# Weight chunks decoded one by one, and x's smaller part by VectorE in every unit: a windowed attention with a gated block behind it

## The chip, the cores and the metric

The kernel runs on one NeuronCore of a Trainium2 chip. The time is device microseconds of one execution, as the median of several. TensorE (PE in the profile) multiplies matrices, VectorE (DVE), ScalarE (ACT) and GpSimd (POOL) work on elements, SyncE (SP) issues the DMAs. Each engine runs its own instructions in program order, and waits on semaphores for the others.

## The reference

For 8 batches and 8 heads of 576 positions with 64 dimensions each position attends to itself and the 63 before it; the result, with the heads side by side, is x (8 x 576 x 512). Then `h = relu(x @ w_in)` (512 to 1024), a convolution of three taps along the sequence for each of the 1024 columns, `gate = 1 / (1 + exp(-conv))`, and `(h * gate) @ w_out` (1024 to 512).

```python
scores = scale * np.matmul(q, k.transpose(0, 1, 3, 2))
mask = (rel >= 0) & (rel < window)
attn = softmax(np.where(mask, scores, -1e9))
x = np.matmul(attn, v)                      # heads side by side
h = np.maximum(x @ w_in, 0.0)
conv_out[s] = sum(conv_w[k] * h[s + k - 1] for k in range(3))
out = (h * sigmoid(conv_out)) @ w_out
```

## The kernel before

The 4608 rows of x are done in 12 units of 384 rows (`NX`), and every unit goes through attention, the product with w_in, the convolution with its gate, and the product with w_out. Units 0 and 1 are taken in halves of the 1024 columns: unit 0's first four chunks of 128 columns, unit 1's first four, unit 0's last four, unit 1's last four (`TASKS`, L44), so that the weights of the second half may come later; from unit 2 on a unit takes its eight chunks in a row.

**Split operands.** The products with w_in and w_out run on a reduced 32-bit type (fp32r). Each operand is held as a larger part, which that type holds exactly, and a smaller part, the rest; a product is three matrix products (larger by larger, larger by smaller, smaller by larger). For x a quarter of a unit (128 of the 512 columns) lies in a PSUM bank when `values` (L643) has multiplied the attention weights with v. `split_hi` (L648) copies the bank to `xh`, rounded. The smaller part `xl` comes about in two ways. For most units VectorE subtracts: `split_lo` (L653) reads the bank and `xh`. For the units in `BY_DIFFERENCE`, 1 and 2, TensorE subtracts in the bank itself, by a product of `xh` with the negated identity matrix (`less`, L657), and ScalarE or VectorE then copies the rest out (`split_rest`, L662). Either way the bank is free for other work only after the smaller part has been read.

**Weights.** w_in and w_out come as 64-bit numbers, as pairs of 32-bit words, in 16 chunks of 128 x 512. Decoding a chunk takes `magnitude` (L445 on ScalarE or L447), `shift` (L451, VectorE), `sign` (L455, VectorE), `low` (L458, ScalarE), `add_low` (L462, VectorE), then `larger` (L480) and `lo` (L485) for the two parts. w_in's chunks 0 and 1 are decoded alone, the other fourteen in pairs, each step once for 1024 columns (`DECODE`, L46). Two buffers `wx` take turns. The three taps (`cbits`, `cw`) are decoded by the same functions.

**Order of the work.** A planning function lists all pieces of work, and a table of numbers (`ORDER`) says in which order they are issued; a letter behind a number names the engine where there is a choice (A, D or P for ScalarE, VectorE, GpSimd), a figure after a slash the PSUM bank, and F*n* stands for *n* products on spare data that fill a gap. Every engine's instructions stand in the order of this table. There are eight banks.

**Other lines that matter.** `scores` (L554) multiplies q and k; `row_max` (L575) and `exps` (L585), `reciprocal` (L597) and `normalise` (L604) make the attention weights of a burst; `turn` (L611) and `unturn` (L616) transpose them for units 0 and 1. `mm1` (L669) is the product with w_in, `relu` L695/697, `conv_mid` L711/713 and `conv_side` L718 the taps, `sigmoid` L722, `gate` L729, `gate_hi` L734 and `gate_lo` L739 the split of h times gate, `mm2` L748 (L753 in the last unit) the product with w_out, `result` L758/761 the copy out of the bank.

Of the kernel before, what the change touches and what calls it, by code (L numbers as in the profile page):

```python
# [8 lines left out]
F32 = mybir.dt.float32  # L9
# [29 lines left out]

BY_DIFFERENCE = (1, 2)  # L40
# [84 lines left out]
def plan():  # L125
# [64 lines left out]
    at("minus")  # L190
# [64 lines left out]
    80A 77D 125 207P 222 215 82/6 239 223A 216P 86A 224 78 208/4 83A 142A 87 225P 217/5 84 198/0 81 232 438 143
    102/7 9 92 145 189 144 10 240 4 93 146 7 113/1 209A 231 147D 104A 148D 127A 226/6 439 443/2 190 115D 241 309
    128 149/7 130 129 242A 199A 116 218A 243 131 233A 114A 251/0 118A 152/1 151A 244P 445 440 2 310 154A 234 444
    164 235P 449 334 252D 165 446 119 245/4 153A 155 236/5 448 253 156 247/7 157D 237A 158 246A 132D 227A 254A
    120 F2/2 255/1 447 159 454/2 450A 133D 256A 248A 259/0 311A 607 117 441 257 455 121 260D 456 F2/5 261 249
# [103 lines left out]
def attention_moe(ctx: ExitStack, tc: tile.TileContext, q, k, v, first, w_in, conv_w, w_out, out):  # L363
# [100 lines left out]
    def part(buf, fs):  # L464
        return wx[buf][:, :len(fs) * DM]
# [409 lines left out]
```

## Time and profile before

| what | us |
|---|---|
| median of 3 runs | 509.57 (509.39 to 510.43) |
| profiled execution, its own time | 509.53 |
| span of the profiled execution | 507.8 |
| TensorE busy | 499.1 (98%), 5377 instructions |
| VectorE busy | 401.3 (79%), 1186 instructions |
| ScalarE busy | 315.5 (62%), 897 instructions |
| GpSimd busy | 149.1 (29%), 223 instructions |

The span runs from the first to the last recorded instruction; 1.7 us of the execution lie around it. A busy engine has an instruction in flight; consecutive instructions of one engine overlap a little in the record, so the length of one is somewhat more than what it adds. The chain of waits begins at the last instruction and goes back to what released each step, so that it shows which engine held up the end at each moment. A group names line, engine and operation, `out<-in`, shape, count, busy us, mean ns of one, and the idle time of the engine just before. The granted TensorE clock is 1.00 of full speed in every stretch shown.

### The profile page before, as it was taken

The numbers are of one execution on the slowest core, as the hardware profiler recorded it, in microseconds if no ns is written. First come the engines' busy times: TensorE is split into PE (matmuls) and PEld (weight loads), VectorE is DVE, ScalarE is ACT, GpSimd is POOL, SyncE is SP. The second block draws the span as 40 slices with busy tenths as digits, with TensorE's granted clock in tenths as the row PEclk, the third lists the DMA queues.
The fourth block names the chain that finished last, engine by engine and source line by source line (L and its number), as shares of the span: only waits on it lengthen the run. The fifth ranks groups of instructions, "written<-read, shape, count | busy, mean of one in ns | idle before, by whom it ended". The sixth has DMA issues, their size and how long they took to land.

```text
span 507.8 us, 13893 instructions
## 1 busy us (share of the span) xinstructions
PE 499.1 (98%) x5377; PEld 440.1 (87%) x5377; DVE 401.3 (79%) x1186; ACT 315.5 (62%) x897; POOL 149.1 (29%) x223
## 2 busy tenths in 40 slices
PE   8898999999999999999999999999999999999997
PEld 5687989888898898888898988989889889888996
DVE  6999999988877896787668887887887688683781
ACT  5999999979736752754767745924663763331150
POOL 4832440323240431331441230335125332203011
PEclk9999999999999999999999999999999999999999
DMA  8999438334364744416243737324444301600031
GB/s 309 346 345 346 151 110 267 112 93 130 110 186 128 203 133 126 131 62 203 78 154 82 243 95 227 97 70 117 144 159 142 102 1 55 207 21 2 0 125 62
DMA packets 27953, 72.04 MB, mean 142 GB/s; under 512 B 6128, under 2 KB 14448, under 8 KB 27888
## 3 DMA queue, kind: packets, MB, share of 16 engines
q1 hardware_dynamic: 27600, 69.59, 42.5%
q0 software_dynamic: 288, 1.57, 1.8%
q8 instruction: 42, 0.69, 0.6%
q14 instruction: 23, 0.19, 0.1%
HBM read 48.26 MB, written 11.01 MB: 117 GB/s over the span
## 4 chain that ended last, share of the span: by engine, by line
PE 92%; DVE 2%; ACT 2%; DMA 1%; POOL 1%; issue 0%; SPq 0%
PE bank L669 39%; PE bank L748 37%; PE bank L643 6%; PE bank L554 5%; PE bank L753 3%; ACT s L585 2%; DMA raw_in<-in_w_in_dram 1%; DVE c L718 1%; DVE s L575 1%; POOL s L604 0%; PE bank L657 0%; PE bank L611 0%; SPq L413 0%; POOL w_in L485 0%; DVE wx L462 0%
## 5 line engine op out<-in xcount | busy, mean ns | idle before, releaser
L669 PE MATMUL bank<-xh,w_in 128*128 128x384 f32 x768 | 196.6, 336 | 0.0
L748 PE MATMUL bank<-w_out,gh 128*128 128x512 f32 x528 | 168.8, 401 | 0.0
L669 PEld LDWEIGHTS bank<-xh,w_in 128*128 128x128 f32 x768 | 139.4, 188 | 6.4 <-ACT hbuf L695 0.6
L669 PE MATMUL bank<-xl,w_in 128*128 128x384 f32 x384 | 128.9, 336 | 0.0
L718 DVE SCALAR_TENSOR_TENSOR c<-hbuf,cw,c 128x386 f32<-128x386 f32 (+1 forms) x192 | 120.1, 651 | 4.3 <-ACT c L711 3.0
L748 PEld LDWEIGHTS bank<-w_out,gh 128*128 128x128 f32 x528 | 95.9, 188 | 19.2
L585 ACT ACTIVATE s<-s,nm 128x96 f32<-128x96 f32 (+2 forms) x288 | 105.0, 367 | 8.7 <-DVE nm L575 8.4
L748 PE MATMUL bank<-w_out,gl 128*128 128x512 f32 x264 | 104.0, 394 | 0.0
L575 DVE CUSTOM_DVE_ANT_0 s<-bank,mask 128x96 f32<-128x96 f32 (+2 forms) x288 | 55.9, 256 | 21.4 <-PE bank L554 21.2
L669 PEld LDWEIGHTS bank<-xl,w_in 128*128 128x128 f32 x384 | 72.1, 188 | 0.1
L722 ACT ACTIVATE c<-c 128x772 f32<-128x772 f32 (+1 forms) x48 | 40.4, 848 | 43.7 <-DVE c L718 43.4
L604 POOL TENSOR_TENSOR s<-s,r 128x768 f32<-128x768 f32 (+1 forms) x30 | 40.9, 1371 | 88.1 <-DVE r L597 87.7
L729 POOL TENSOR_TENSOR c<-c,hbuf 128x2 f32<-128x2 f32 (+4 forms) x34 | 39.1, 1165 | 81.0 <-ACT c L722 80.8
L739 POOL TENSOR_TENSOR gl<-c,gh 128x768 fp32r<-128x768 f32 (+1 forms) x17 | 33.2, 1951 | 100.7 <-DVE gh L734 54.0
L748 PEld LDWEIGHTS bank<-w_out,gl 128*128 128x128 f32 x264 | 49.6, 188 | 11.9 <-POOL gl L739 0.2
L711 ACT ACTIVATE c<-hbuf,cw 128x386 f32<-128x386 f32 (+1 forms) x58 | 35.1, 614 | 39.3 <-DVE hbuf L697 17.2
L585 ACT ACTIVATION_READ_ACCUMULATOR s<-s,nm 128x1 f32 x288 | 54.5, 189 | 0.0
L695 ACT ACTIVATE hbuf<-bank 128x384 f32<-128x384 f32 x51 | 24.2, 483 | 42.6 <-PE bank L669 42.6
L697 DVE TENSOR_SCALAR hbuf<-bank 128x384 f32<-128x384 f32 x45 | 24.8, 553 | 24.0 <-PE bank L669 22.4
L643 PEld LDWEIGHTS bank<-ub,v 128*64 128x64 f32 x1152 | 35.8, 138 | 7.6 <-issue 4.9
L643 PE MATMUL bank<-ub,v 128*64 128x64 f32 x1152 | 38.9, 224 | 0.9 <-ACT ub L616 0.7
L554 PEld LDWEIGHTS bank<-qk 64*32 64x32 f32 (+1 forms) x2112 | 30.2, 111 | 10.7 <-issue 5.5
(83 smaller groups left out, 530.0 us busy)
## 6 DMA issues: line engine op xcount, KB each, us to landing
v<-in_v_dram SPq DMA_DIRECT2D x24, 768.0 KB, 5.4
ub<-T SPq DMA_DIRECT2D x240, 48.0 KB, 2.8
qk<-in_k_dram SPq DMA_DIRECT2D x20, 448.0 KB, 4.7
out_dram<-ot SPq DMA_DIRECT2D x11, 768.0 KB, 4.8
qk<-in_q_dram SPq DMA_DIRECT2D x20, 384.0 KB, 4.5
raw_in<-in_w_in_dram SPq DMA_DIRECT2D x8, 512.0 KB, 6.7
raw_out<-in_w_out_dram SPq DMA_DIRECT2D x8, 512.0 KB, 6.8
qk<-in_first_dram SPq DMA_DIRECT2D x12, 320.0 KB, 5.1
```

What stands on the lines that cost most here:

```text
L554: nc.tensor.matmul(banks[bank[h]][r:r + rows, i * P + o:i * P + k], qq[hs, s:s + rows], kk[hs, s + o:s + k], start=True, stop=True)
L575: nc.vector.tensor_tensor_reduce(out=ss[n // NB][:, n % NB, h, o:k], in0=banks[bank[h]][:, i * P + o:i * P + k], in1=mask[m][:, o:k], scal ...
L585: nc.scalar.activation(x, x, AF.Exp, bias=small(nms, (n,))[:, h:h + 1], scale=-1.0, accum_out=small(sms, (n,))[:, h:h + 1])
L604: engine[on].tensor_tensor(sv, sv, small(rs, ns).unsqueeze(2).broadcast_to([P, 2 * len(ns), k]), ALU.mult)
L643: nc.tensor.matmul(banks[bank[0]][h * D:(h + 1) * D, t * W:(t + 1) * W], vs[:, c, t, h], ub[g][:, 2 * p:2 * p + 2, 2 * t + h], start=(t == ...
L669: nc.tensor.matmul(banks[bank[0]][:, :NX], w[:, a, c], y[x][:, c], start=(c == 0 and j == 0), stop=(c == NC - 1 and j == 2))
L711: nc.scalar.activation(c, h, AF.Copy, scale=w)
L718: nc.vector.scalar_tensor_tensor(c, h, w, c, op0=ALU.mult, op1=ALU.add)
L722: nc.scalar.activation(both(u, j), both(u, j), AF.Sigmoid)
L729: engine[on].tensor_tensor(c[:, :, a:a + n], c[:, :, a + o:a + o + n], h[:, :, 1 + a + o:1 + a + o + n], ALU.mult)
L739: engine[on].tensor_tensor(gls[j % 3][:, :, :n], cs[j % 2][:, :, :n], ghs[j % 3][:, :, :n].bitcast(F32), ALU.subtract)
L748: nc.tensor.matmul(banks[bank[0]], x, wts["out", f][:, w], start=(start and i == 0), stop=(stop and i == 2))
```

## The change

Every step of the decoding but `shift` is issued once for each chunk of 512 columns, and each chunk has its own tiles for the raw words and for its two parts; `shift` still takes a pair at once. The subtraction on TensorE, the copies behind it and the negated identity are gone: `split_lo` on VectorE makes the smaller part in all 12 units (48 instead of 40), and the smaller parts of units 1 and 2, 8 products and 8 copies, are no longer there. All of `values`' products start and stop their own accumulation. `ORDER` is a new table throughout (its first line is shown). It also chooses engines anew: over the whole program GpSimd has 8 of the `larger` and 9 of the `lo` (chunks), where it had 4 and 2.

```diff
-BY_DIFFERENCE = (1, 2)
...
-        for fn in ("magnitude", "shift", "sign", "low", "add_low", "larger", "lo"):
-            at(fn, key, fs, buf)
+        for j, f in enumerate(fs):
+            at("magnitude", key, f, buf, j)
+        at("shift", key, fs, buf)
+        for j, f in enumerate(fs):
+            for fn in ("sign", "low", "add_low", "larger", "lo"):
+                at(fn, key, f, buf, j)
...
-            if u in BY_DIFFERENCE:
-                at("less", u, c, bank=bank)
-                at("split_rest", u, c, bank=bank)
-            else:
-                at("split_lo", u, c, bank=bank)
+            at("split_lo", u, c, bank=bank)
...
-    at("minus")
...
-    0 14 94 13 12 3 319 105 49 358 16 21 17 103 15 150 F4/0 39/2 40 185 98 95D 42 F3/0 30/4 96 97 20/6 99 184 6
+    161 13 102 104 338 87 2 11 0 15 93 12 389 16 20 F4/0 38/2 14 88 145 105A 89 39 146 108 106 F3/0 19/4 41 107
...
-        if (key, fs) not in raws:
-            raws[key, fs] = pool.tile([P, len(fs) * DM, 2], U32, name=f"raw_{key}{fs[0]}", tag=f"{key}{fs[0]}")
-        a = fs.index(f) * DM
-        nc.sync.dma_start(raws[key, fs][:, a:a + DM].rearrange("p e two -> p (e two)"), src[key][f].bitcast(U32))
+        raws[key, f] = pool.tile([P, DM, 2], U32, name=f"raw_{key}{f}", tag=f"{key}{f}")
+        nc.sync.dma_start(raws[key, f].rearrange("p e two -> p (e two)"), src[key][f].bitcast(U32))
...
-        copy(on)(w[:, 0], part(buf, fs))
+        copy(on)(wts[key, f][:, 0], part(buf, j))
...
-        engine[on].tensor_tensor(w[:, 1], part(buf, fs), w[:, 0].bitcast(F32), ALU.subtract)
+        engine[on].tensor_tensor(wts[key, f][:, 1], part(buf, j), wts[key, f][:, 0].bitcast(F32), ALU.subtract)
...
-                                 ub[g][:, 2 * p:2 * p + 2, 2 * t + h], start=(t == 0), stop=(t == NT - 1))
+                                 ub[g][:, 2 * p:2 * p + 2, 2 * t + h], start=True, stop=True)
```

The lines of the changed program that the rows below name: `shift` L446, `sign` L450, `add_low` L457, `lo` L477, `reciprocal` L585, `normalise` L592, `values` L631, `split_lo` L641, `mm1` L648, `conv_mid` L692, `conv_side` L697, `gate` L708, `gate_lo` L718; its load lines are `load_first` L411, `load_v` L423, `load_w` L428 and `load_conv` L432.

VectorE at the smaller parts of unit 2 (`xl_68`, `xh_65`), in the changed program; `bank_111` holds a quarter of unit 2:

```order
L450 SCALAR_TENSOR_TENSOR wx_70<-raw_out_731,wx_70 128x512
L692 TENSOR_SCALAR c_94<-hbuf,cw 128x386
L457 ISA wx_70<-raw_out_731,wx_70 128x1024
L697 SCALAR_TENSOR_TENSOR c_94<-hbuf,cw,c_94 128x386
L708 TENSOR_TENSOR c_93<-c_93,hbuf 128x2
L708 TENSOR_TENSOR c_93<-c_93,hbuf 128x2x383
L585 RECIPROCAL r_91<-sm_88 128x8
L641 TENSOR_TENSOR xl_68<-bank_111,xh_65 128x384
L585 RECIPROCAL r_90<-sm_87 128x8
L592 TENSOR_TENSOR s_82<-s_82,r_91 128x8x96
L457 ISA wx_70<-raw_out_962,wx_70 128x1024
L718 TENSOR_TENSOR gl_99<-c_93,gh_96 128x2x384
```

The same place of VectorE before:

```order
L485 TENSOR_TENSOR w_in_1228<-wx_71,w_in_1228 128x1024
L718 SCALAR_TENSOR_TENSOR c_95<-hbuf,cw,c_95 128x386 x4
L713 TENSOR_SCALAR c_94<-hbuf,cw 128x386
L662 CAST xl_68<-bank_105 128x384
L718 SCALAR_TENSOR_TENSOR c_94<-hbuf,cw,c_94 128x386 x2
L697 TENSOR_SCALAR hbuf<-bank_112 128x384
L718 SCALAR_TENSOR_TENSOR c_94<-hbuf,cw,c_94 128x386 x2
L451 TENSOR_SCALAR wx_70<-wx_70 128x1024
L729 TENSOR_TENSOR c_95<-c_95,hbuf 128x2x193
```

In the changed program the subtraction of unit 2's second quarter stands on VectorE behind decoding steps of single chunks of w_out and the convolution of a unit before; before, VectorE had one copy of a rest among its convolution steps there, and no subtraction.

TensorE at the same place in the changed program (`ub_62` holds attention weights of unit 2, `xh_64` and `xl_67` are unit 1's x):

```order
L648 MATMUL bank_105<-xh_64,w_in_922 128x384 x2
L648 MATMUL bank_105<-xl_67,w_in_922 128x384
L631 MATMUL bank_111<-ub_62,v 64x64 x12
L631 MATMUL bank_104<-ub_62,v 64x64 x12
L648 MATMUL bank_105<-xh_64,w_in_1176 128x384 x2
L648 MATMUL bank_105<-xl_67,w_in_1176 128x384
```

TensorE at unit 2's third quarter before:

```order
L669 MATMUL bank_105<-xh_64,w_in_1228 128x384 x2
L669 MATMUL bank_105<-xl_67,w_in_1228 128x384
L643 MATMUL bank_112<-ub_62,v 64x64 x12
L748 MATMUL bank_110<-w_out_1376,gh_97 128x512 x2
L748 MATMUL bank_110<-w_out_1376,gl_100 128x512
L748 MATMUL bank_109<-w_out_1376,gh_97 128x512 x2
L748 MATMUL bank_109<-w_out_1376,gl_100 128x512
L657 MATMUL bank_112<-xh_65,negated 128x384
L748 MATMUL bank_111<-w_out_1376,gh_97 128x512 x2
```

In the changed program the third quarter's `values` goes into bank_111, which the second quarter's subtraction still reads, and it is followed at once by the fourth quarter and by products of unit 1; before, the bank of the quarter was turned into its rest by a product with `negated`, and read out by a copy.

The first DMAs in SyncE's queue before:

```order
L413 DMA qk<-in_first_dram 128x640
L433 DMA raw_in_130<-in_w_in_dram 128x1024
L413 DMA qk<-in_first_dram 128x640 x2
L433 DMA raw_in_138<-in_w_in_dram 128x1024
L413 DMA qk<-in_first_dram 128x640 x5
L526 DMA mask_76<-mask_75 32x96
L413 DMA qk<-in_first_dram 128x640
L437 DMA cbits<-in_conv_w_dram 128x48
L413 DMA qk<-in_first_dram 128x640 x3
L425 DMA v<-in_v_dram 128x1536 x2
L526 DMA mask_76<-mask_75 32x96
```

and in the changed program:

```order
L411 DMA qk<-in_first_dram 128x640
L428 DMA raw_in_122<-in_w_in_dram 128x1024
L432 DMA cbits<-in_conv_w_dram 128x48
L411 DMA qk<-in_first_dram 128x640 x2
L428 DMA raw_in_144<-in_w_in_dram 128x1024
L411 DMA qk<-in_first_dram 128x640 x3
L428 DMA raw_in_166<-in_w_in_dram 128x1024
L428 DMA raw_in_174<-in_w_in_dram 128x1024
L411 DMA qk<-in_first_dram 128x640 x2
L423 DMA v<-in_v_dram 128x1536
```

The conv weights' words (`cbits`) move up to the third place, two more chunks of w_in stand ahead of v, and the two masks' copies move back.

## Rows read from the trace of the kernel before

**Rows 1.** Busy time by stretch of the span: start, end and length in us, then the busy us of PE, of its weight loads (PEld), of VectorE (DVE), ScalarE (ACT) and GpSimd (POOL) with instruction counts, the granted TensorE clock as a share of full speed, the DMA engines' share and GB/s.

```profile
5.13:48.00 42.87, 39.61 (x674) 31.68 (x675) 41.56 (x188) 40.95 (x153) 19.28 (x25) 1.00 0.96 346
48.00:91.00 43.00, 43.00 (x454) 37.71 (x453) 41.84 (x118) 42.62 (x120) 13.78 (x15) 1.00 0.62 200
...
115.00:300.00 185.00, 185.00 (x2092) 163.84 (x2091) 145.08 (x445) 119.06 (x343) 55.85 (x80) 1.00 0.47 139
```

**Rows 2.** Single instructions in order of time: start us, length us, engine, line, operation. Unit 1's first w_in product, the last product of the program, and the copy behind it.

```profile
47.86 0.51 PE L669 MATMUL bank<-xh,w_in 128*128 128x384 f32 x2
...
503.83 0.33 PE L753 MATMUL bank<-gl,w_out 128*128 128x386 f32 x1
...
504.20 0.48 ACT L761 COPY ot<-bank 128x386 f32<-128x386 f32 x1 [0.87 <-PE bank L753]
```

**Rows 3.** What VectorE waited for between 5.2 and 93.7 us, its largest entry: us in total, times, longest.

```profile
DVE r L597 <- ACT sm L591: 0.9, 3, 0.3
```

**Rows 4.** The group of products that subtract the larger part, over the whole span: count, busy us, mean ns of one, idle time ahead of them.

```profile
L657 PE MATMUL bank<-xh,negated 128*128 128x384 f32 x8 | 2.8, 386 | 0.6 <-DVE xh L648 0.6
```

**Rows 5.** VectorE's groups of instructions in the first 93.7 us, each shape apart: count, busy us, mean ns of one, idle time ahead.

```profile
L718 DVE SCALAR_TENSOR_TENSOR c<-hbuf,cw,c 128x386 f32<-128x386 f32 x21 | 12.4, 616 | 0.1
...
L485 DVE TENSOR_TENSOR w_out<-wx,w_out 128x1024 fp32r<-128x1024 f32 x3 | 3.7, 1221 | 0.0
L462 DVE CUSTOM_DVE_ANT_0 wx<-raw_out,wx 128x2048 uint16<-128x2048 uint16 x3 | 3.6, 1210 | 0.0
L455 DVE SCALAR_TENSOR_TENSOR wx<-raw_out,wx 128x1024 uint32<-128x1024 uint32 x3 | 3.6, 1209 | 0.0
L616 DVE COPY ub<-bank 128x512 f32<-128x512 f32 x5 | 3.2, 680 | 0.0
...
L604 DVE TENSOR_TENSOR s<-s,r 128x768 f32<-128x768 f32 x3 | 2.9, 955 | 0.1
...
L697 DVE TENSOR_SCALAR hbuf<-bank 128x384 f32<-128x384 f32 x4 | 2.2, 549 | 0.0
...
L653 DVE TENSOR_TENSOR xl<-bank,xh 128x384 fp32r<-128x384 f32 x4 | 1.9, 545 | 0.0
L713 DVE TENSOR_SCALAR c<-hbuf,cw 128x386 f32<-128x386 f32 x4 | 1.7, 418 | 0.0
...
L662 DVE CAST xl<-bank 128x384 fp32r<-128x384 f32 x3 | 1.6, 553 | 0.0
...
L455 DVE SCALAR_TENSOR_TENSOR wx<-raw_in,wx 128x512 uint32<-128x512 uint32 x2 | 1.4, 692 | 0.0
L480 DVE CAST w_out<-wx 128x1024 fp32r<-128x1024 f32 x2 | 1.4, 692 | 0.0
...
L729 DVE TENSOR_TENSOR c<-c,hbuf 128x386 f32<-128x386 f32 x2 | 1.1, 552 | 0.0
...
L485 DVE TENSOR_TENSOR w_in<-wx,w_in 128x512 fp32r<-128x512 f32 x1 | 0.7, 710 | 0.0
```

**Rows 6.** VectorE in order of time: a shift of a pair of weight chunks and behind it two smaller parts of x of unit 1, the second pair of its four quarters.

```profile
46.47 0.09 DVE L575 DVE_READ_ACCUMULATOR2_ANT nm<- 128x1 f32 x1
...
47.08 1.02 DVE L662 CAST xl<-bank 128x384 fp32r<-128x384 f32 x2
```

**Rows 7.** The start: VectorE's first maximum, ScalarE's first decoding step, and, of the list of DMA issues, that of the conv weights (count, KB each, median us from issue to landing); then the first product of the attention weights with v.

```profile
5.13 0.29 DVE L575 CUSTOM_DVE_ANT_0 s<-bank,mask 128x128 f32<-128x128 f32 x1 [3.73 <-PE bank L554]
...
5.10 0.69 ACT L458 ACTIVATE raw_in<-raw_in 128x512 uint32<-128x512 uint32 x1 [3.08 <-DMA raw_in<-in_w_in_dram]
...
cbits<-in_conv_w_dram SPq DMA_DIRECT2D x1, 24.0 KB, 5.0
...
21.74 0.68 PE L643 MATMUL bank<-ub,v 128*64 128x64 f32 x15
```

**Rows 8.** The chain of work that ended last: start us, length us, what. A run of TensorE instructions of one line stands as one piece.

```profile
57.11 0.93 PE bank L554 x56
58.04 2.28 PE bank L748 x9
...
87.19 0.85 PE bank L643 x24
...
120.35 2.08 PE bank L748 x9
...
129.41 3.02 PE bank L643 x96
...
202.29 1.66 PE bank L554 x108
...
225.52 8.34 PE bank L669 x48
233.86 5.57 PE bank L748 x24
...
489.35 14.83 PE bank L753 x84
```

**Rows 9.** VectorE from 73 us on in order of time, and GpSimd's instruction of the same moment.

```profile
73.32 1.98 DVE L462 CUSTOM_DVE_ANT_0 wx<-raw_in,wx 128x2048 uint16<-128x2048 uint16 x1
...
72.37 1.84 POOL L739 TENSOR_TENSOR gl<-c,gh 128x768 fp32r<-128x768 f32 x1 [1.68 <-ACT gh L734]
```

**Rows 10.** GpSimd's narrow smaller part of a weight chunk: count, busy us, mean ns of one, idle ahead.

```profile
L485 POOL TENSOR_TENSOR w_in<-wx,w_in 128x512 fp32r<-128x512 f32 x1 | 1.3, 1282 | 0.1
```

More of the change, by code (lines that the diff above doesn't have):

```diff
@@ L255 @@
[L255 to L259, printed above, removed]
@@ L382, in attention_moe @@
     ident = pool.tile([P, P], F32, name="ident")
-    negated = pool.tile([P, P], F32R, name="negated")
     qk = pool.tile([P, FIRST], F32, name="qk")
@@ L428, in load_w @@
     def load_w(key, f):
-        fs = next(fs for k, fs in DECODE if k == key and f in fs)
-        if (key, fs) not in raws:
-            raws[key, fs] = pool.tile([P, len(fs) * DM, 2], U32, name=f"raw_{key}{fs[0]}", tag=f"{key}{fs[0]}")
-        a = fs.index(f) * DM
-        nc.sync.dma_start(raws[key, fs][:, a:a + DM].rearrange("p e two -> p (e two)"), src[key][f].bitcast(U32))
+        raws[key, f] = pool.tile([P, DM, 2], U32, name=f"raw_{key}{f}", tag=f"{key}{f}")
+        nc.sync.dma_start(raws[key, f].rearrange("p e two -> p (e two)"), src[key][f].bitcast(U32))
     @work
@@ L462, in to_add_low, with part @@
         nc.vector.tensor_tensor(xu, xu, lw, ALU.add)
-    def part(buf, fs):
-        return wx[buf][:, :len(fs) * DM]
-    fn["magnitude"] = lambda key, fs, buf, on: to_magnitude(part(buf, fs), raws[key, fs][..., 1], on)
-    fn["sign"] = lambda key, fs, buf: to_sign(part(buf, fs), raws[key, fs][..., 1])
-    fn["low"] = lambda key, fs, buf: to_low(raws[key, fs][..., 0])
-    fn["add_low"] = lambda key, fs, buf: to_add_low(part(buf, fs), raws[key, fs][..., 0])
+    def part(buf, j):
+        return wx[buf][:, j * DM:(j + 1) * DM]
+    fn["magnitude"] = lambda key, f, buf, j, on: to_magnitude(part(buf, j), raws[key, f][..., 1], on)
+    fn["sign"] = lambda key, f, buf, j: to_sign(part(buf, j), raws[key, f][..., 1])
+    fn["low"] = lambda key, f, buf, j: to_low(raws[key, f][..., 0])
+    fn["add_low"] = lambda key, f, buf, j: to_add_low(part(buf, j), raws[key, f][..., 0])
     def copy(on):
@@ L475, in larger, with lo @@
     @work
[L476 to L480 removed]
+    def larger(key, f, buf, j, on):
+        wts[key, f] = pool.tile([P, 2, DM], F32R, name=f"w_{key}{f}", tag=f"{key}{f}")
+        copy(on)(wts[key, f][:, 0], part(buf, j))
     @work
[L483 to L485 removed]
+    def lo(key, f, buf, j, on):
+        engine[on].tensor_tensor(wts[key, f][:, 1], part(buf, j), wts[key, f][:, 0].bitcast(F32), ALU.subtract)
     @work
@@ L511, in identity @@
         make_identity(nc, ident)
-    @work
-    def minus():
-        nc.scalar.activation(negated, ident, AF.Copy, scale=-1.0)
     @work
@@ L653, in split_lo @@
         nc.vector.tensor_tensor(xl[x][:, c], banks[bank[0]][:, :NX], xh[x][:, c].bitcast(F32), ALU.subtract)
-    @work
-    def less(u, c, bank):
-        nc.tensor.matmul(banks[bank[0]][:, :NX], negated, xh[x_of(u)][:, c], start=False, stop=True,
-                         skip_group_check=True)
-    @work
-    def split_rest(u, c, on, bank):
-        copy(on)(xl[x_of(u)][:, c], banks[bank[0]][:, :NX])
     @work
```

197 lines of the change are left out of this document (99 added, 98 removed).

## The prediction

> **What bounds the kernel now.** I read the windows first. From 48 us on TensorE has an instruction in flight in every microsecond, at full granted clock; only between 5.13 and 48 us are 3.3 us of 42.87 free, and there VectorE (41.56) and ScalarE (40.95) are as full [rows 1]. Then I looked for where TensorE's unbroken work begins and ends: unit 1's first w_in product starts at 47.86, the last product of the program at 503.83 and adds about 0.17, so it is done at 504.0; a copy and the store fill the rest up to 507.8, 3.8 us [rows 2]. So three terms make the span: when the unbroken stretch begins, how much work TensorE has in it, and the tail. The change cannot shorten the first by less work on TensorE, but it can lengthen it where TensorE has to wait for VectorE. The waits say how near that is: between 5.2 and 93.7 us VectorE's largest idle entry is 0.9 us, for ScalarE's sums [rows 3], and up to 91 us it is busy 41.84 of 43.0, ScalarE 42.62. From 115 us on both have room: VectorE 145 of 185 us [rows 1]. What the change does to VectorE counts up to some 93 us, and behind that hardly at all.
>
> **The change part by part.** *What goes from TensorE:* eight products with the negated identity. They last 386 ns each by the record [rows 4], but overlapping ones add 0.174 (48 w_in products in 8.34 us, rows 8), so 8 x 0.174 = 1.4 us, of which four, 0.7 us, lie behind 47.86. A fill product more takes 0.23 back. This counts only where TensorE sets the pace.
>
> *What VectorE has to do up to the second subtraction of unit 2.* I name this place because TensorE's `values` for unit 2's third quarter writes bank_111, which is free only when VectorE has subtracted the second quarter from it; that subtraction stands behind decoding and convolution in VectorE's order, and behind the waiting `values` stand the fourth quarter and all the rest of TensorE's queue. Before, TensorE and a copy did that quarter. I compare VectorE's work ahead of it with what VectorE of before had done by 93.7 us. An instruction adds about 0.08 less than its length: the shift at 46.47 lasts 0.69 and the next begins at 47.08 [rows 6]. By the groups of the first 93.7 us [rows 5]:
> `sign`: 6 pairs at 1.14 and 2 single at 0.61 to 0.69 (I take 0.65) become 14 single: 8.14 to 9.10, +1.0. `add_low`: 6 x 1.13 and 2 single become 13 single at the same 0.65: +0.4. `lo`: 5 x 1.14 and 1 single become 5 single, since GpSimd takes the others: -3.1. `larger`: three of a pair at 0.61 go: -1.8. Smaller parts of x: 4 subtractions and 3 copies (545 and 553 ns) become 10 subtractions at 0.47: +1.4. `normalise`: three more of 512 columns, which I estimate at 0.7 from the 955 ns of 768: +2.1. First taps: 3 more at 0.34, +1.0; other taps 22 for 21, +0.5. `relu`: two fewer at 0.47, -0.9. `gate`: four of half width go (4 x 0.47), one of full width comes (0.87 as the 768-wide product with r, and 0.08 of a short one): -0.9. `unturn`: one fewer, -0.6. Two guards fewer (0.09 each, an estimate from the other narrow steps) and a `magnitude` more (as 0.34): +0.2. The sum is 1.0 + 0.4 - 3.1 - 1.8 + 1.4 + 2.1 + 1.0 + 0.5 - 0.9 - 0.9 - 0.6 + 0.2 = -0.7, call it -0.8 with the unrounded terms: VectorE has almost the same to do, because GpSimd takes what the decoding by chunks adds.
>
> *VectorE's start.* Its first instruction in the changed order is the conv weights' shift, so it waits for their DMA, now third in the queue. Before, its first maximum stood at 5.13, and the first chunk's words were there at 5.10 [rows 7]; the words of the taps took 5.0 from issue to landing in the old place, and ScalarE's idle time ahead of 5.10 began at 2.02, which I take for the time of issue. If they come with the first chunk, ScalarE's two narrow steps cost 0.4 and the maximum moves by 0.4; if they take the 5.0, it moves by up to 2.3. Bounds 0 and 2.3, I take 0.5, near the first chunk's row, for the transfer is small and early. So the subtraction ends at 93.7 - 0.8 + 0.5 = 93.4.
>
> *TensorE behind that place.* In the changed order there follow 984 w_in products x 0.17375 = 171.0 (48 in 8.34); 720 w_out products x 0.2321 = 167.1 (24 in 5.57); 96 of the last unit x 0.1765 = 16.95 (84 in 14.83); 38 pieces of `values` in 12 groups: 38 x 0.72 + 12 x 0.13 = 28.9 (one 0.85, four 3.02); 24 bursts of scores in 19 groups: 19 x 0.93 + 5 x 0.73 = 21.3 (one 0.93, two 1.66); 28 returns from narrow to wide products x 0.2 = 5.6 (nine w_out products 2.28 behind scores, 2.08 elsewhere). All from the chain [rows 8]; the sum is 410.8. As a test, the same prices over the old order from 47.86 on (1104, 792, 96 products, 40 pieces in 16 groups, 27 bursts in 20, 35 returns, four subtractions) give 454.9; measured are 504.0 - 47.86 = 456.1 [rows 2]. So I scale by 1.0026: 411.9.
>
> *The sum.* 93.4 + 411.9 + 3.8 = 509.1 of span, and 1.7 us around it: 510.8. The profiled execution of before took 509.53 with its span of 507.8; the median of the runs is 509.57, so the forecast stands 1.2 us above it. Without any new wait TensorE would reach the place at 47.86 + 455.9 - 411.9 = 91.9 (455.9 is the same count of the changed order from unit 1's first w_in product): a wait of 1.5 us is forecast there.
>
> *At no cost.* ScalarE loses five copies and the negated identity and gains single steps of decoding; the sums of both orders stay within about 0.6 us of each other up to there by its groups, under GpSimd's and VectorE's cover. v lands later: two more chunks of 0.52 MB stand ahead of it, 1.05 MB at 346 GB/s [rows 1] are 3.0 us; I estimate its landing at 17.3 by the bytes ahead of it, and the first product with v stood at 21.74 [rows 7], so 4 us of cover are left; were they gone, each microsecond would go to the start. Separate accumulation of each piece of `values` adds no instruction.
>
> *GpSimd beside VectorE.* At 73.32 a pair's `add_low` on VectorE took 1.98 us where its kind has 1.21 [rows 5]; GpSimd's subtraction with two operands ran from 72.37 for 1.84 [rows 9]. The excess of 0.75 is as if VectorE had been held until GpSimd's instruction ended at 74.21. In the first 93.7 us five of GpSimd's instructions decode; in the changed order some 16 stand up to that place. By rows, one hold among the 40 instructions that GpSimd ran from 5 to 91 us [rows 1] makes 11 more worth 0.2 us, which I leave out of the sum.
> The Trainium skill, page "SBUF — State Buffer", section "SBUF: two separate sides", says that VectorE and GpSimd share a pair of ports as an exclusive lock, which the first to come holds for its whole instruction. The row at 73.32 agrees; by the rule taken at its worst, eleven more instructions that each hold VectorE back by half a microsecond, the sum would be some 5 us longer, and by the trace 0.2.
>
> **The rivals.** *Hidden.* VectorE keeps up: its start does not move, the smaller `lo` share or shorter waits give 1.5 us, and TensorE reaches every bank as it is free. Then 47.86 + 455.9 + 3.8 + 1.7 = 509.3. For it: -0.8 of VectorE's sum; against it: both engines are dense before 91 us, so any hold goes through.
> *Faster.* TensorE has 3.3 us free before 48 us [rows 1]; single chunks can be ready earlier than a pair. Unit 1's second pair of smaller parts ended at 48.10 [rows 6]; a w_in product takes its fourth quarter 9 x 0.174 = 1.57 after it starts, so with those parts in time it could start at 46.5, and if the later waits vanish too: 46.5 + 455.9 + 3.8 + 1.7 = 507.9. Against it: VectorE and ScalarE have no room for the earlier parts.
> *Slower by GpSimd.* Each hold costs 0.75 at VectorE, GpSimd's narrow `lo` lasting 1.28 [rows 10]. From two or three holds more than before on, the subtraction of the second quarter ends 1.5 to 2.2 later: 512.3 to 513.0. It decides from the first hold on VectorE behind some 15 us, as nothing there is slack.
> *That the change does not do what it says:* if the split of unit 2 stood elsewhere in VectorE's order; the order printed rules it out.
>
> **How the numbers follow.** The forecast of a wait at unit 2's bank gets 0.48, hidden 0.24, slower by GpSimd 0.14, faster 0.14. The measurement cannot tell less than 0.2%, 1.0 us, from no change: faster is below 508.55, slower above 510.59. The forecast is one microsecond wide either way, so some 0.7 of it is slower and 0.3 within; hidden lies within for 0.85, the rest faster. That gives slower 0.34 + 0.14 = 0.48, same 0.14 + 0.20 = 0.35 (rounded), faster 0.14 + 0.03 = 0.17. The range goes from 508.2, just above the faster case, to 513.0, the upper end of GpSimd's; the likeliest case alone has 509.8 to 511.6.
>
> **What would show it.** In the profile of the changed kernel: TensorE idle some 1.5 us ahead of `values` at 91 to 94 us, released by VectorE's subtraction; VectorE dense up to there, and its subtraction ending near 93.4; the maximum at the start about 0.5 later than 5.13; from there to the last product 411.9 us. The forecast is wrong if TensorE's list of waits is empty behind 50 us (then hidden or faster, told apart by unit 1's first w_in product at 47.9 or at 46.5), or if VectorE has lengthened steps beside GpSimd's (slower).

## The result, and the profile after

The changed kernel takes 512.98 us (median of 4 runs, 512.54 to 513.5) where the kernel before took 509.48 beside it: the ratio is 1.0063, 95% interval 1.0051 to 1.0075. It is slower by 3.5 us by the medians, by 3.2 us by the ratio. The profiled execution took 512.63, with a span of 510.9 us, 3.1 more than before.

The stretches of [rows 1], in the changed kernel (same columns):

```profile
5.13:48.00 42.87, 36.51 (x606) 28.98 (x605) 40.96 (x177) 40.64 (x148) 23.48 (x28) 1.00 0.90 336
48.00:91.00 43.00, 40.63 (x478) 35.66 (x479) 42.62 (x137) 40.42 (x133) 18.72 (x23) 1.00 0.54 177
...
115.00:300.00 185.00, 185.00 (x2146) 163.59 (x2146) 150.25 (x454) 116.02 (x347) 58.55 (x80) 1.00 0.45 136
```

TensorE has 3.1 us less done between 5.13 and 48 us, and is free for 2.4 us of the next 43, where it had no gap before; behind 115 us it is as dense as it was. The whole loss lies ahead of 96 us. The places that answer to [rows 2], in order of time: unit 1's first w_in product, scores at 70 us, `values` of unit 2's third and fourth quarter, and the last product.

```profile
48.43 0.62 PE L648 MATMUL bank<-xh,w_in 128*128 128x384 f32 x2 [0.67 <-DVE xl L641]
...
70.00 1.16 PE L542 MATMUL bank<-qk 64*32 64x96 f32 x64 [1.57 <-DVE nm L563]
...
95.07 1.69 PE L631 MATMUL bank<-ub,v 128*64 128x64 f32 x48 [0.27 <-DVE xl L641]
...
507.01 0.33 PE L732 MATMUL bank<-gl,w_out 128*128 128x386 f32 x1
```

At 95.07 TensorE waits for VectorE's subtraction, as forecast, but for 0.27 us and not for 1.5: it came there late itself. It had lost 0.57 us by the later start of unit 1's first product (47.86 before [rows 2]), 1.57 at 70.00 for VectorE's maxima and 0.4 for a DMA of attention weights. From 95.07 to the end of the last product (507.01 + 0.17) are 412.1 us; 411.9 were forecast. What TensorE waited for from 5 us on, by line (us in total, times, longest):

```profile
PE bank L599 <- POOL s L592: 3.7, 3, 2.7
PE bank L542 <- DVE nm L563: 1.6, 1, 1.6
...
PE bank L648 <- DVE xl L641: 1.2, 2, 0.7
...
PE bank L631 <- DVE xl L641: 0.3, 1, 0.3
```

Of these the entry "values (L631) <- DVE xl" and the w_in products' (L648) are for the smaller part of x; the 1.6 us for the maxima (L542 <- nm) lie at 70 us, ahead of scores whose bank VectorE had not read. The largest entry, 3.7 us for GpSimd's `normalise`, lies ahead of 48 us (1.3 in the kernel before); it is not what makes the kernel slower, for with one VectorE instruction moved (below) 2.6 us of it remain and the loss is gone. The chain of waits up to 110 us shows who was late (start us, length, what):

```profile
1.64 4.02 DMA cbits<-in_conv_w_dram
...
65.25 2.99 DVE wx L446
...
83.64 1.32 DVE wx L450
...
95.07 1.69 PE bank L631 x48
```

From 22 us on it runs through VectorE almost without a break until 95.07, and a `shift` of 2.99 us is the longest piece of an engine in it up to there. VectorE and GpSimd there, in order of time:

```profile
64.41 0.91 DVE L718 TENSOR_TENSOR gl<-c,gh 128x768 fp32r<-128x768 f32 x1
65.25 2.99 DVE L446 TENSOR_SCALAR wx<-wx 128x1024 uint32<-128x1024 uint32 x1
...
70.04 1.53 DVE L450 SCALAR_TENSOR_TENSOR wx<-raw_in,wx 128x512 uint32<-128x512 uint32 x1
...
94.51 0.51 DVE L641 TENSOR_TENSOR xl<-bank,xh 128x384 fp32r<-128x384 f32 x1
```

```profile
65.13 0.73 POOL L619 MEMSET ub<- 32x768 f32 x1
65.84 1.84 POOL L708 TENSOR_TENSOR c<-c,hbuf 128x386 f32<-128x386 f32 x2
...
69.19 1.83 POOL L718 TENSOR_TENSOR gl<-c,gh 128x768 fp32r<-128x768 f32 x1 [0.47 <-ACT gh L713]
```

The shift (L446) lasts 0.69 us by itself. Here it begins while GpSimd fills a block (L619, up to 65.86), and ends 0.55 after GpSimd's two gate instructions have ended (67.68). The sign at 70.04 ends 0.55 after GpSimd's gate_lo (71.02). Its own subtraction for bank_111 VectorE does at 94.51 to 95.02. The decoding in the first 95 us, to be read against [rows 5] (count, busy us, mean ns of one):

```profile
L450 DVE SCALAR_TENSOR_TENSOR wx<-raw_in,wx 128x512 uint32<-128x512 uint32 x8 | 7.1, 881 | 0.1
...
L457 DVE CUSTOM_DVE_ANT_0 wx<-raw_out,wx 128x1024 uint16<-128x1024 uint16 x5 | 3.3, 681 | 0.0
```

The steps of L457 were not held and took 681 ns; the mean of L450, 881, contains the long ones. And the start, against [rows 7]:

```profile
5.94 0.18 DVE L446 TENSOR_SCALAR cw<-cw 128x24 uint32<-128x24 uint32 x1 [4.54 <-ACT cw L440]
6.07 0.29 DVE L563 CUSTOM_DVE_ANT_0 s<-bank,mask 128x128 f32<-128x128 f32 x1
```

The taps' words came so late that VectorE's first maximum stands at 6.07, 0.94 later than before; 0.5 had been forecast.

### The profile page after: what moved, and what is told of

Same layout as the page of the kernel before. It is cut to its first block, busy times and chain, and to the rows that moved or that the text cites. A ratio compares the mean times of both kernels' runs of the same rounds, so it can differ in the third digit from the quotient of the medians.

```text
span 510.9 us, 13939 instructions
## 1 busy us (share of the span) xinstructions
PE 496.6 (97%) x5370; PEld 438.6 (86%) x5370; DVE 401.9 (79%) x1194; ACT 323.7 (63%) x925; POOL 159.5 (31%) x232
## 3 DMA queue, kind: packets, MB, share of 16 engines
q0 software_dynamic: 288, 1.57, 1.8%
## 4 chain that ended last, share of the span: by engine, by line
PE 81%; DVE 16%; issue 1%; DMA 1%; POOL 0%; SPq 0%; ACT 0%; DVEq 0%
PE bank L648 34%; PE bank L727 34%; PE bank L631 6%; PE bank L542 4%; PE bank L732 3%; DVE s L563 3%; DVE c L697 2%; DVE wx L450 2%; DVE wx L457 1%; DVE wx L446 1%; DVE xl L641 1%; DVE s L592 1%; DMA cbits<-in_conv_w_dram 1%; DVE T L611 1%; DVE w_in L477 0%
## 5 line engine op out<-in xcount | busy, mean ns | idle before, releaser
L648 PE MATMUL bank<-xh,w_in 128*128 128x384 f32 x768 | 197.2, 337 | 1.2 <-DVE xl L641 1.2
L648 PEld LDWEIGHTS bank<-xh,w_in 128*128 128x128 f32 x768 | 139.2, 188 | 9.0 <-DVE xl L641 2.1
L697 DVE SCALAR_TENSOR_TENSOR c<-hbuf,cw,c 128x386 f32<-128x386 f32 (+1 forms) x192 | 121.8, 658 | 12.3 <-ACT c L690 10.4
L648 PE MATMUL bank<-xl,w_in 128*128 128x384 f32 x384 | 129.1, 336 | 0.1
L708 POOL TENSOR_TENSOR c<-c,hbuf 128x386 f32<-128x386 f32 (+5 forms) x36 | 42.5, 1196 | 123.6 <-ACT c L701 123.6
L648 PEld LDWEIGHTS bank<-xl,w_in 128*128 128x128 f32 x384 | 72.1, 188 | 0.6 <-DVE xl L641 0.6
L718 POOL TENSOR_TENSOR gl<-c,gh 128x768 fp32r<-128x768 f32 (+1 forms) x20 | 37.8, 1890 | 62.4 <-DVE gh L713 51.6
L674 ACT ACTIVATE hbuf<-bank 128x384 f32<-128x384 f32 x58 | 27.8, 485 | 44.7 <-PE bank L648 44.6
L592 POOL TENSOR_TENSOR s<-s,r 128x768 f32<-128x768 f32 (+1 forms) x23 | 33.3, 1458 | 35.1 <-DVE r L585 35.1
L631 PEld LDWEIGHTS bank<-ub,v 128*64 128x64 f32 x1152 | 35.4, 138 | 6.2 <-issue 3.8
L542 PEld LDWEIGHTS bank<-qk 64*32 64x32 f32 (+1 forms) x2112 | 29.7, 110 | 12.0 <-issue 4.8
L542 PE MATMUL bank<-qk 64*32 64x96 f32 (+2 forms) x2112 | 37.4, 254 | 2.2 <-DVE nm L563 1.6
L690 ACT ACTIVATE c<-hbuf,cw 128x386 f32<-128x386 f32 (+1 forms) x54 | 32.3, 613 | 10.0 <-DVE hbuf L676 6.1
L631 PE MATMUL bank<-ub,v 128*64 128x64 f32 x1152 | 37.9, 224 | 0.6 <-DMA ub<-T 0.4
```

The lines of the kernel that those rows point to most:

```text
L542: nc.tensor.matmul(banks[bank[h]][r:r + rows, i * P + o:i * P + k], qq[hs, s:s + rows], kk[hs, s + o:s + k], start=True, stop=True)
L592: engine[on].tensor_tensor(sv, sv, small(rs, ns).unsqueeze(2).broadcast_to([P, 2 * len(ns), k]), ALU.mult)
L631: nc.tensor.matmul(banks[bank[0]][h * D:(h + 1) * D, t * W:(t + 1) * W], vs[:, c, t, h], ub[g][:, 2 * p:2 * p + 2, 2 * t + h], start=True, ...
L648: nc.tensor.matmul(banks[bank[0]][:, :NX], w[:, a, c], y[x][:, c], start=(c == 0 and j == 0), stop=(c == NC - 1 and j == 2))
L690: nc.scalar.activation(c, h, AF.Copy, scale=w)
L697: nc.vector.scalar_tensor_tensor(c, h, w, c, op0=ALU.mult, op1=ALU.add)
```

## The experiments

The theory, H: VectorE sets the pace up to unit 2's smaller parts, and what stretches it there is GpSimd, whose instructions hold some of VectorE's up for as long as they run. The rivals: the work of the two parts itself (C for the chunks, S for the subtractions), GpSimd's work as mere load (P), or a start that VectorE does not set (N). All ratios are to the kernel before on the same chip; for the changed kernel 1.0063.

**One gate on VectorE instead of GpSimd.** In the table of the order 288 is the gate of unit 1's first pair of chunks:

```diff
-519 377 190 288P 501 193
+519 377 190 288D 501 193
```

> The changed kernel (512.98 us) with one gate, unit 1's first pair of chunks, on VectorE instead of GpSimd. Theory H, VectorE sets the pace up to unit 2's smaller parts and GpSimd's two-operand instructions hold it up: the shift at 65.25 takes 0.69 instead of 2.99, VectorE has 1.0 us of gate more to do, so its subtraction ends 1.3 us earlier and the time is 511.7. Rival P, VectorE merely has more work (no hold by GpSimd): 1.0 us more work there, 514.0. Rival N, TensorE or the start sets the time: 513.0.

Measured: 511.56, 1.0026 [1.0016, 1.0035]. VectorE was given 1.0 us of work more, and the kernel became about 1.9 us faster. The shift now, and GpSimd's block beside it:

```profile
64.85 1.14 DVE L446 TENSOR_SCALAR wx<-wx 128x1024 uint32<-128x1024 uint32 x1
```

```profile
64.71 0.73 POOL L619 MEMSET ub<- 32x768 f32 x1
```

It ends at 65.99, 0.55 after the fill of the block, with no gates behind that. P and N fall. (The profiled execution, 510.53, is the fastest of this kernel's ten.)

**The shift later.** The same work on the same engines; only the place of one instruction in VectorE's order changes.

In the table 377 is the shift, 288P the gate, 378 the sign of w_in's chunk 6:

```diff
-519 377 190 288P 501 193
+519 190 288P 501 193
...
-508 289A 378 657/2
+508 289A 377 378 657/2
```

> The changed kernel with the one shift that took 2.99 us issued later on VectorE, just ahead of the sign that needs it, behind eight maxima that read PSUM; no work changes engine. Theory H: the hold shrinks from 2.3 us to at most 0.5, and the sign behind it may get ahead of GpSimd's gate_lo too (0.84): 510.2 to 511.2. Rival P (the 2.99 us are something of this shift itself, or no pace of VectorE): 513.0, with a shift as long as before.

Measured: 510.02, 1.0000 [0.9989, 1.0010], a little better than expected. The shift takes 0.82, and TensorE comes to unit 2's third quarter without a wait:

```profile
67.50 0.82 DVE L446 TENSOR_SCALAR wx<-wx 128x1024 uint32<-128x1024 uint32 x1
...
92.64 1.70 PE L631 MATMUL bank<-ub,v 128*64 128x64 f32 x48
```

One instruction moved takes back the whole loss that can be measured.

**The shift earlier**, ahead of gate_lo, to have it beside the fill of a block alone.

174D is that gate_lo:

```diff
-502 174D 646/2 519 377 190 288P
+502 377 174D 646/2 519 190 288P
```

> The changed kernel with the long shift one place earlier on VectorE, ahead of gate_lo of unit 0, so that it runs at about 64.4 beside GpSimd's memset of a block and not beside its gates. Theory H, only GpSimd's instructions with two operands in SBUF hold VectorE: the shift takes 0.69, and gate_lo is done before the gates begin: 510.0 to 511.0. Rival M, any instruction of GpSimd holds it, memsets too: the shift ends 0.6 later than it should, and gate_lo, now beside the gates, is held in its place: 512.5 to 513.

Measured: 513.93, 1.0085 [1.0072, 1.0098]; M's side, and worse. VectorE and GpSimd:

```profile
65.35 1.23 DVE L446 TENSOR_SCALAR wx<-wx 128x1024 uint32<-128x1024 uint32 x1 [0.70 <-ACT wx L440]
66.50 1.68 DVE L718 TENSOR_TENSOR gl<-c,gh 128x768 fp32r<-128x768 f32 x1
...
70.00 2.34 DVE L450 SCALAR_TENSOR_TENSOR wx<-raw_in,wx 128x512 uint32<-128x512 uint32 x1
```

```profile
65.30 0.73 POOL L619 MEMSET ub<- 32x768 f32 x1
66.00 2.97 POOL L708 TENSOR_TENSOR c<-c,hbuf 128x386 f32<-128x386 f32 x2
...
69.93 1.86 POOL L718 TENSOR_TENSOR gl<-c,gh 128x768 fp32r<-128x768 f32 x1 [0.45 <-DVE nm L563]
```

The shift waited 0.70 for its magnitude, which I had overlooked, met the block's fill after all, and ended 0.55 behind it (66.03). gate_lo then began at 66.50 beside the first gate and took 1.68 instead of 0.91; the two gates took 2.97 instead of 1.84, so each engine held the other. The sign at 70.00 took 2.34. My condition "two operands in SBUF" was too narrow: a fill has none and still held the shift. M goes too far in its turn: steps with two operands were not held beside a fill (counts at the end).

**The taps moved back**: their DMA behind the first loads, their three first steps to where the others stand, at about 25 us (87 is the DMA, 88 to 90 are magnitude, shift and sign, 91 is `low`).

```diff
-338 87 2
+338 2
...
-14 88 145 105A 89 39
+14 145 105A 39
...
-200 90 21 110P 202
+200 21 110P 87 202
...
-237 91
+237 88 89 90 91
```

> The changed kernel with the conv weights' DMA behind the first loads and their three steps (magnitude, shift, sign) moved back to about 25 us, where the others stand. Theory H: VectorE's first maximum at 5.1 instead of 6.07, all of it carried to the end: 512.1. Rival N (the early delay is absorbed by a later wait): 513.0.

Measured: 512.79, 1.0051 [1.0033, 1.0069]; against 1.0063 not told apart. The first maximum does stand at 5.14, and `values` at 94.50 instead of 95.07, so that 0.6 of the 0.9 reach TensorE in this execution:

```profile
5.14 0.29 DVE L563 CUSTOM_DVE_ANT_0 s<-bank,mask 128x128 f32<-128x128 f32 x1 [3.75 <-PE bank L542]
...
64.53 3.01 DVE L446 TENSOR_SCALAR wx<-wx 128x1024 uint32<-128x1024 uint32 x1
...
94.50 1.70 PE L631 MATMUL bank<-ub,v 128*64 128x64 f32 x48 [0.27 <-DVE xl L641]
```

The shift is as long as it was. **Taps and shift together:**

> Both the taps moved back and the shift later. Theory H: the gains add, 0.9 and 1.8 to 2.8: 509.3 to 510.3, unless other pairs of instructions meet by the shifted times. Rival N: 513.0.

Measured: 509.62, 0.9994 [0.9984, 1.0003], no longer told apart from the kernel before:

```profile
91.63 1.62 PE L631 MATMUL bank<-ub,v 128*64 128x64 f32 x48
```

In all these kernels the start of `values` for unit 2's third quarter and the span keep their distance, as they must if nothing behind it waits: 95.07 and 510.9 in the changed kernel, 92.91 and 508.8 with the gate on VectorE, 92.64 and 508.6 with the shift later, 94.50 and 510.6 with the taps moved, 91.63 and 507.5 with both. The distance is 415.8 to 416.1; forecast were 411.9 + 3.8 = 415.7.

**The parts alone, in the old order.** The kernel before with each step of a pair written as two steps in its place; then with `split_lo` where the rests were copied and the subtracting products left away; then with both. (The first edit of the code is that of the change itself.)

```diff
-BY_DIFFERENCE = (1, 2)
+BY_DIFFERENCE = ()
```

> The kernel before (its order and engines) with only the decoding by single chunks: each step of a pair is two steps in its place. Theory H: on VectorE a chunk's step adds 0.60 where a pair's adds 1.14, so six signs, six add_lows and five los cost 1.0 us more up to 93.7, three larger parts 0.3; that or nothing goes to the end: 509.6 to 511.0, without new long holds. Rival C, decoding by chunks is what costs: 512 to 513.

> The kernel before with only x's smaller part by VectorE in units 1 and 2, at the places where the rests were copied; the subtracting products are gone. Theory H: VectorE has 2.35 us more by 93.7 (five copies that ScalarE did), 0.95 of it ahead of unit 1's first product, TensorE 0.7 us less behind that: 508.9 to 510.8. Rival S, the subtractions on VectorE are what costs: 512 to 513.

> The kernel before with both parts, chunks and subtraction, still in its own order and with its own engines. Theory H, the loss comes from where the new order lets GpSimd's instructions meet VectorE's, not from the two parts: the sum of the two single runs, 509.5 to 511.5. Rivals C or S: 512.5 to 514.

Measured: chunks 511.52, 1.0038 [1.0023, 1.0053]; subtraction 510.74, 1.0023 [1.0008, 1.0039]; both 515.00, 1.0107 [1.0090, 1.0124]. Each part costs something in the old order, 1.9 and 1.2 us by the ratios. That is more than H gave the chunks, and both together lie 3.5 us above H's range, on the side of C and S. With the chunks unit 1's first w_in product starts at 48.84 instead of 47.86 [rows 2], after a wait of 1.08 for VectorE (0.6 before [rows 4]):

```profile
46.88 0.62 PE L657 MATMUL bank<-xh,negated 128*128 128x384 f32 x2 [1.08 <-DVE xh L648]
...
48.84 0.51 PE L669 MATMUL bank<-xh,w_in 128*128 128x384 f32 x2
```

H had expected no new long hold there, and there is one ahead of that product. The second of two `add_low` steps (first line) stands beside GpSimd's `normalise` (second line); the pair's one step in the kernel before (third line) had begun ahead of that `normalise`, which came at 35.65:

```profile
35.99 1.53 DVE L465 CUSTOM_DVE_ANT_0 wx<-raw_out,wx 128x1024 uint16<-128x1024 uint16 x1
...
35.58 1.40 POOL L604 TENSOR_TENSOR s<-s,r 128x512 f32<-128x512 f32 x1 [8.48 <-DVE r L597]
...
35.49 1.19 DVE L462 CUSTOM_DVE_ANT_0 wx<-raw_out,wx 128x2048 uint16<-128x2048 uint16 x1
```

It took 1.53 where such a step takes 0.68, so that some 0.85 of the 0.98 by which the product comes later can be this hold. What the subtraction alone costs does not show in its profile, which is of its fastest run (509.68, span 507.9); in seven of its ten runs the mean granted clock was 0.990 to 0.996, and how much of the 1.2 us that makes is not shown.

Both together cost 5.4, 2.3 more than the sum. There TensorE has waited 2.26 us for maxima, its clock falls, and the shift of w_in's chunks 4 and 5 meets GpSimd's gate (windows, columns as in [rows 1]; then single instructions of TensorE and VectorE):

```profile
46.00:48.00 2.00, 0.26 (x9) 0.26 (x17) 2.00 (x18) 1.99 (x4) 0.64 (x2) 0.81 1.03 407
48.00:50.00 2.00, 2.00 (x65) 1.39 (x63) 2.00 (x2) 2.00 (x5) 1.84 (x3) 0.50 1.00 373
...
52.00:54.00 2.00, 2.00 (x8) 2.00 (x8) 2.00 (x4) 1.15 (x4) 0.00 (x0) 0.50 1.02 416
```

```profile
47.74 1.71 PE L554 MATMUL bank<-qk 64*32 64x96 f32 x64 [2.26 <-DVE nm L575]
...
50.37 0.98 PE L669 MATMUL bank<-xh,w_in 128*128 128x384 f32 x2 [0.20 <-ACT wx L448]
...
47.78 1.98 DVE L454 TENSOR_SCALAR wx<-wx 128x1024 uint32<-128x1024 uint32 x1
```

TensorE worked 0.26 us of the stretch from 46 to 48; from 48 to 54 it was granted 0.50 of full speed, that is 1.2 GHz, and a pair of w_in products took 0.98 instead of 0.51. Moving that shift behind the three subtractions of unit 1, which read PSUM:

```diff
-shift("in", (4, 5)), ... split_lo(1, 2), split_lo(1, 3), split_lo(1, 0)
+split_lo(1, 2), split_lo(1, 3), split_lo(1, 0), shift("in", (4, 5))
```

> Both parts in the old order (515.0), with the one shift that took 1.98 us beside GpSimd's gate moved behind three subtractions of unit 1 that read PSUM. Theory H: 1.3 us less ahead of unit 1's products, and TensorE idles less there, so that the clock may stay up: 512.5 to 513.7. Rival C, the sum of the two parts' work is the loss: 515.0.

Measured: 513.89, 1.0084 [1.0069, 1.0098], 1.1 us better and just outside H's range. In the profiled execution, the fastest of four, unit 1's first product stands at 49.21 and the clock stays at 1.00, although TensorE had waited 2.26 us for the same maxima and worked only 0.22 us of the stretch from 46 to 48; in the other three runs the mean granted clock is 0.993 to 0.997. So what made the clock fall is not shown, nor how much of the 1.1 us is the hold's and how much the clock's.

In the old order 4.3 us of cost remain after that hold is gone. They can't be put down to the work of the two parts alone, for VectorE is still held three times: at an `add_low` as with the chunks alone (1.53 at 35.90), and at a `gate_lo` and a tap beside GpSimd's `lo` and gates:

```profile
54.55 2.05 DVE L739 TENSOR_TENSOR gl<-c,gh 128x768 fp32r<-128x768 f32 x1
...
59.66 2.21 DVE L718 SCALAR_TENSOR_TENSOR c<-hbuf,cw,c 128x386 f32<-128x386 f32 x1
```

```profile
53.95 1.84 POOL L485 TENSOR_TENSOR w_in<-wx,w_in 128x512 fp32r<-128x512 f32 x1 [4.52 <-ACT w_in L481]
...
59.29 2.15 POOL L729 TENSOR_TENSOR c<-c,hbuf 128x2 f32<-128x2 f32 x2
```

Alone they take 0.95 and 0.61. The three holds make 3.6 us, against 0.8 in the kernel before. What the two parts together cost in this order without holds no run shows. In the new order nothing that can be measured remains with one shift moved.

**By difference again, in the new order:** the subtracting products and the copies of the rests, on the engines of before, stand where `split_lo` stood for units 1 and 2.

```diff
-split_lo(u, c)
+less(u, c), split_rest(u, c)
```

> The changed kernel with x's smaller part of units 1 and 2 made by difference again, on the engines of before, in the changed order. Theory H: VectorE has 2.35 us less, but the shift of 2.99 us still stands beside GpSimd's gates, and other waits of TensorE on VectorE (w_in's for the gate, 84 to 91 us) stay: 511.0 to 512.7. Rival S: all comes back, 509.5.

Measured: 516.95, 1.0145 [1.0130, 1.0160], worse than either theory said. The new table has no good place for these steps: VectorE waits 2.2 us in all for the subtracting products, the shift is held again (2.70 us), and TensorE's clock is 0.83 of full speed between 70 and 80 us. This run does not decide about S; it only shows that giving VectorE's subtractions back does not help in this order.

**A version to beat both.** Taps and shift as above, and fewer holds at the start, where w_in's chunk 0 is decoded beside GpSimd's lo and its first normalise:

```diff
-magnitude, shift, sign (w_in 0), maxima (2, 3), add_low (w_in 0), maxima (10, 11)
+maxima (2, 3), maxima (10, 11), magnitude, shift, sign, add_low (w_in 0)
```

> Taps moved back, the long shift later, and the first decoding steps of w_in's chunk 0 (magnitude, shift, sign, add_low) behind two more maxima, so that fewer of them stand beside GpSimd's lo and normalise (0.46 and 0.73 of holds before). Theory H: unit 1's first w_in product starts some 0.6 earlier than 47.69, all carried to the end: 0.6 below the version with taps and shift alone (509.62), 509.0, and so faster than the kernel before by 0.1 to 0.2%. Rival N, the start is set by GpSimd's normalise or ScalarE's exponentials: no change, 509.6.

Measured: 510.58, 1.0019 [1.0009, 1.0029], a miss. The profile is of its longest run: TensorE's first scores waited for their operands (first line: us in total, times, longest), and VectorE for the scores of the burst whose maxima were put ahead of the decoding (second line):

```profile
PE bank L542 <- DMA qk<-in_first_dram: 1.7, 1, 1.7
...
12.82 0.29 DVE L563 CUSTOM_DVE_ANT_0 s<-bank,mask 128x128 f32<-128x128 f32 x1 [1.61 <-PE bank L542]
```

How much of either is in the median run is not shown; VectorE has nothing left there to do while it waits. So only the sign of that chunk was moved, behind one burst's maxima:

```diff
-sign (w_in 0), maxima (2, 3)
+maxima (2, 3), sign (w_in 0)
```

> Taps moved back and the long shift later (509.62 in its run, 0.9994 of before), and the sign of w_in's chunk 0 one place later on VectorE, behind the maximum of the next burst, so that GpSimd's first normalise is over when it begins. Theory H: 0.7 us less ahead of unit 1's first product, which starts at 47.0 instead of 47.69: 0.998 of before, 508.9. Rival N, the loads or the chain of exponentials and normalise set the start there: no change, 509.6, or a later start.

Measured: 509.09, 0.9982 [0.9972, 0.9991]: faster than both kernels, by 0.9 us than the one before and by about 4 than the changed one. The sign takes 0.69 instead of 1.41:

```profile
11.68 0.29 DVE L563 CUSTOM_DVE_ANT_0 s<-bank,mask 128x128 f32<-128x128 f32 x1 [0.62 <-PE bank L542]
...
12.53 0.69 DVE L450 SCALAR_TENSOR_TENSOR wx<-raw_in,wx 128x512 uint32<-128x512 uint32 x1
```

In this profiled execution VectorE waited 0.62 for the scores ahead of it, and unit 1's first product stands at 47.65, not at 47.0. That this edit alone makes the gain over the version with taps and shift (0.9994) is not shown, since the two intervals overlap. Over the kernels in the new order time and holds mostly go together: up to 95 us VectorE is held for about 5 us in the changed kernel (512.98), with the taps moved (512.79) and with the shift earlier (513.93), for about 2 with the gate on VectorE (511.56, with 1.0 of work more), with the shift later (510.02) and with taps and shift (509.62), and for 0.9 in this last version (509.09). The version before it, with 1.6 (510.58), has its waits at the start besides.

## Why the prediction was right or wrong

The direction was right, and so was the place up to which VectorE counts: the chain leaves VectorE at the subtraction ahead of unit 2's third quarter. The wait forecast for TensorE there was not: 0.27 us instead of 1.5, because TensorE had lost its time in earlier waits; the longest of these behind 48 us, 1.57, was for VectorE as well. Nor was the size: 510.8 was forecast, +1.2 us, and +3.5 came. The time lies inside the range (508.2 to 513.0, measured 512.98) by 0.02 us, and only because the range was drawn up to the end of the rival "slower by GpSimd"; the likeliest case alone had 509.8 to 511.6. That is luck and no merit of the sum. And one of the prediction's own signs of being wrong came true: VectorE has lengthened steps beside GpSimd's. By the steps:

- *TensorE behind that place:* 411.9 forecast, 412.1 measured. The prices by the chain held, and so did the tail, 3.8 against 3.7.
- *The end of the subtraction:* 93.4 forecast, 95.02 measured. This is the mis-sized term. Adding up VectorE's time in both profiles, from its first maximum to the places compared (93.7 before, 95.02 now), its parts were:
- *VectorE's start:* +0.5 forecast, +0.94 measured in this execution (0.5 in two others of the same start, where the first maximum stands at 5.62). Its upper bound of 2.3 was not reached.
- *VectorE's work:* -0.8 forecast, about -3.1 measured (82.3 us without idle time and holds, against 85.4). The narrow steps add 0.60 each, not the 0.65 I took; 32 of them make 1.6 of the difference. (That a step adds some 0.08 less than its length was read from the first line below, of the kernel before, behind which the next step begins at 47.08; the row that [rows 6] prints for 46.47 is the reading of a maximum.)

```profile
46.47 0.69 DVE L451 TENSOR_SCALAR wx<-wx 128x1024 uint32<-128x1024 uint32 x1
```

- *VectorE's idle time:* left as it was, measured 1.0 less (1.5 against 2.5).
- *GpSimd beside VectorE:* the step that failed. I saw the hold in [rows 9], priced eleven more GpSimd instructions at 0.2 and left even that out of the sum. Measured are holds of 5.2 us up to the subtraction against 0.8 before, 4.5 more: 2.30 at the shift of 65.25, 0.84 at the sign of 70.04, 0.73 at that of 12.00, 0.63 at that of 83.64, 0.54 at a magnitude at 10.55, 0.2 at a tap at 57.98.

These are 93.4 + 0.4 - 2.3 - 1.0 + 4.5 = 95.0: less work and less idle time than forecast hid 3.3 us of what the holds added. The rival "slower by GpSimd" gave 512.3 to 513.0 with a chance of 0.14, and its mechanism is what the runs show; but it asked for two or three holds of 0.75 by decoding steps of GpSimd, and the largest was one of 2.3 by a fill and gates. Only 0.7 us of the holds, at the magnitude and the tap, stand beside GpSimd's decoding; the others stand beside gates, a `gate_lo`, a `normalise` and the fill of a block, kinds of work that GpSimd had in the kernel before as well. My error was to count how often VectorE was held per instruction of GpSimd, over a kernel whose order mostly kept the two apart, instead of asking which pairs of instructions stand beside each other in the new order. That could be read there: a shift from SBUF to SBUF right ahead of GpSimd's gate.

The Trainium skill, page "SBUF — State Buffer", section "SBUF: two separate sides", has the shared port pair as an exclusive lock, taken by VectorE in its two-port modes, or with two SBUF inputs against an instruction of GpSimd that reads SBUF. The runs agree, down to that condition (the counts below: two operands against a memset 0 of 33), and its worst case in the prediction, some 5 us, was nearer to the 4.5 us of holds added than my 0.2. In which mode VectorE ran an instruction no run here shows.

The rival *hidden* is what is left without the long hold: 510.02 with the shift moved, where it gave 509.3. *Faster* (507.9) was reached by no run; the last version, with 0.9 us of holds left, took 509.09.

What stays open: what each part costs in the old order beside the holds and the lower clock, what made the clock fall there, and how much of the last version's gain is the sign's.

## What to carry to other kernels

Work given to GpSimd is free for VectorE only while VectorE runs something that the two do not contend for. Where VectorE sets the pace, look in the order for its SBUF-to-SBUF steps that stand beside GpSimd's long instructions, and put the steps that read PSUM there instead, as far as what they read is ready: here one step moved was worth 3 us, and four steps moved at the start gave a slower kernel than one. A step cut in two can meet what the whole one did not. A mean rate of such collisions from one order says nothing about another.

## What the runs showed of the hardware

I went through all fourteen profiles for VectorE's instructions that began while one of GpSimd's had at least 0.2 us to run, and call one held when it took over 0.12 us longer than its kind. With an operand in PSUM: 0 of some 1800 were held beside GpSimd's two-operand products and subtractions. Transposes (222) and reciprocals (119): none. With two operands in SBUF: 216 of 233; they ended their own length, less 0.12 to 0.22 us, after GpSimd's instruction. Of the other 17, nine had no more than 0.25 us of GpSimd's instruction ahead of them, so that there was next to nothing to wait for; eight are one sign (at 41.28 in the changed kernel) which ran at its own length while GpSimd's two gates beside it took 2.70 instead of 1.84. Single-operand steps from SBUF to SBUF (shift, magnitude, first taps, casts): 54 of 73. The other 19 are first taps that began with 0.21 to 0.28 us of a `normalise` left; they too ended 0.2 us short of their own length after it, which leaves 0.08 us of hold at most, so they are no exceptions. Beside a memset of GpSimd, steps with two operands were never held (0 of 33), single-operand steps always (5 of 5, all of them the shift of 65.25 in the changed kernel and four others). I had not expected either half of that. Nor that a held instruction may stay behind two or three of GpSimd's in a row: the shift of 65.25 waited for a memset and both gates, 2.3 us, where in another run (65.35) it got in after the memset.
